# A chunked recurrence with an MLP behind it: the first superstep's triangular inverse in two halves, a second engine that issues DMAs, and a new instruction order

## The chip, the cores and the metric

The kernel runs on one core of one Trainium2 chip. The metric is the device time of one execution in microseconds; the kernel before was run three times (853.11, 855.16 and 856.32 us, median 855.16). A further execution was taken with the hardware profiler. Engines: PE multiplies matrices (into PSUM), DVE, ACT and POOL work element by element, SP issues DMAs. Each engine runs its own instructions strictly in the order in which they were emitted and waits on semaphores for the others.

## The reference

For 4 batches and 8 heads a state of 40x40 goes through 768 time steps; then an MLP with its weights in float64 works on all 3072 tokens:

```python
for t in range(S):
    y[:, :, t] = np.einsum('bhd,bhde->bhe', rt, state)
    Sa = np.einsum('bhde,bhe->bhd', state, at)
    state_decay = state * wt[:, :, None, :] - np.einsum('bhd,bhe->bhde', Sa, bt)
    state = state_decay + np.einsum('bhd,bhe->bhde', vt, kt)
...
x = y.transpose(0, 2, 1, 3).reshape(3072, 320)
h = x @ w_in                                  # 320 x 2048
sp = np.maximum(h, 0.0) + np.log1p(np.exp(-np.abs(h)))
out = (h * erf(sp)) @ w_out                   # 2048 x 320
```

## The kernel before, in words

**Tiling.** The 32 recurrences are worked in two groups of 16, the 768 steps in 6 supersteps of 128 steps, each of 4 chunks of 32 steps. A group's superstep is called q (q0 to q11, the two groups in turn, the second six chunks behind); q0c3 is chunk 3 of the first superstep of the first group. Inside a chunk the recurrence is written as matrix products and one triangular 32x32 solve for each head, so that only the state passes from chunk to chunk.

**Stages of a superstep.**
- `prep` (line 635): a DMA brings the decays w; two scans on DVE (lines 649 and 653) make suffix products (tile Wt) and prefix products (tile Pr).
- `aphase` (662), for each chunk: a DMA (kba) brings k, b and a; `ab` and `bk` (684, 689; DVE or POOL) scale them by the products; `A` (694) makes the chunk's scores on PE in the PSUM tile pA; `Am` (701) masks them into the chunk's Zs tile; two DMAs (AD) write a part of them to DRAM for another layout; `bT` (712) transposes bk through pA, and `bTc` copies that to an sg tile. There are 11 Zs and 11 sg tiles, so scores can be made 11 chunks ahead.
- `tphase` (718), once for all four chunks: DMAs (Ti, Ap) fetch the scores from DRAM, 128 partitions with one 16x16 triangle each; two ACT fills set its border; 14 pairs of a multiply `Tm` (741) and a subtract `Ts` (742) on DVE invert it in place; DMAs write it back (TD) and load it as 32x32 blocks (tb); `R` (750) transposes on DVE; `W` and `DAD` on PE (757) with `Wm` (761) and `Tb` (764) on DVE make the remaining quarter of each block.
- `chain` (767), for each chunk in turn: `Z` (800), the solve `U` (809), copies to SBUF (lines 587 and 589), small DMAs (zu; in q0 copies `zmu`), `PQ` (845) and its mask (848), `MY` (856, 860), and then the new state MT (863) and the outputs Ym (867), which go to DRAM (xw) after chunk 3.
- The MLP for 256 tokens: `load_x` (986) reads the outputs back (xr) and splits them into a high and a low float32r part (xh, xl); `mm1` (1021) makes h out of eight float32r products; `tanh`, `ln`, `exp`, `gelu` on ACT (1029), `nd`, `rho`, `E`, `G` (1053, 1054, 1065, 1066) on DVE or POOL make the activation; `mm2` (1075) multiplies by w_out; `ob` and `out` write the result.
- `weights` (927): 20 DMAs (wd) of float64 weights, each turned into float32 by six instructions (lines 947 to 952: w1 = L947, w3 = L948 and w5 = L952 on DVE, w5 also on POOL; the rest on ACT), those of w_in split into two float32r parts (956, 957, 977, 978).

**The order.** The code only lists operations: `P.add` records name, engine, tiles read and written. The list ORDER (line 17) says in which sequence all 4418 operations are emitted, and the string ENGINES (line 203) gives each its engine: P for PE, A for ACT, V for DVE, G for POOL, S for SP. The lists came out of a planner (`Plan.schedule`, line 303), which is run again only if their lengths don't fit the number of operations. An entry of -1 in ORDER is a filler: a bfloat16 matmul of no use (line 595) that keeps PE at work; there are 288. All 907 DMAs have the letter S:

```python
def dma(self, name, o, i, rd=(), wr=(), pr=0):
    self.P.add(name, "SP", lambda e: self.eng(e).dma_start(o(), i()), rd, wr, pr, ISSUE.get(name, 0.41))
```

For q0, which has no earlier work to hide behind, `aphase` borrows tiles that are not yet in use: chunks 1 to 3 take their kba into Pr[1], Pr[2] and VT[1], and chunks 1 and 3 their scaled a into T. The order within the first microseconds is: a first weight load, the identity, w.q0, kba of chunk 0, and so on; the kba of chunks 2 and 1, and then 3, come later among weight loads.

Of the kernel before, what the change touches and what calls it, by code (L numbers as in the profile page):

```python
# [7 lines left out]
F32 = mybir.dt.float32  # L8
# [7 lines left out]
SCRATCH = 512  # L16
ORDER = (
# [228 lines left out]
LSC = -(0.5 - 2.0 ** -24)  # L246


TICK = 10.24 / 3
FETCH, BLOCK, PHASE = 3.6, 127.3, 94.9  # L250
PAIRS = dict(W=32, DAD=32, mm1=8, mm2=2, A=16, PQ=16, Z=32, U=32, MY=64, pmt=4, UT=2, bT=4, cT=1)
# [9 lines left out]
class Plan:  # L261
# [41 lines left out]
    def schedule(self):  # L303
# [57 lines left out]
        while done < n:  # L361
# [5 lines left out]
            for i in avail:  # L367
                o = ops[i]
                best = None
                for e, d, k in o["alts"]:  # L370
                    if k and lock > now + 1e-9:
                        continue
# [715 lines left out]
def build(tc, I, out, K={}, D=13.5, Dm=27.0, lag=0.0, t0=60.0, amargin=55.0, wpr=40.0, vlag=3.0, tmargin=10.0, verbose=False, emit=True, seq=False, check=True):  # L1088
    with ExitStack() as ctx:
# [17 lines left out]
        def tph(q):  # L1107
            N.tphase(*N.steps[q], pq(q) + 15)
# [117 lines left out]
```

## Time and profile before

| | |
|---|---|
| median of 3 runs (lowest, highest) | 855.16 us (853.11, 856.32) |
| the profiled execution: its time | 849.49 us |
| its span, first to last instruction | 847.7 us |
| mean granted TensorE clock | 0.966 |
| DMA packets; those under 512 bytes | 211459; 165132 |
| DMA bytes, mean rate | 98.96 MB, 117 GB/s |

How to read the views. The page gives for each engine its busy time and its share of the span; a busy PE includes the fillers. The windows give the same for stretches of the span. A row of the timeline is: start, duration, engine, source line, operation, tiles (output<-inputs), shapes, count, and in brackets how long the engine had been idle and who released it. The chain of work that ended last is followed back from the end of the program, at each step to what released it; its rows are start, duration, engine, output tile and line. Rows of DMA issues give count, then shortest, median and longest duration of the issue in ns; that is the time of the issuing engine, not of the transfer. All times below come from the one profiled execution.

### The profile page before, as it was taken

How to read it: one execution, taken by the hardware profiler on the slowest of the kernel's cores; microseconds unless marked ns; L12 is line 12 of the kernel's file. 1: busy time of each engine (PE TensorE's matmuls, PEld its weight loads, DVE VectorE, ACT ScalarE, POOL GpSimd, SP SyncE). 2: the span in 40 equal slices, each digit the busy share in tenths (PEclk: the TensorE clock that was granted, in tenths of full speed). 3: DMA queues.
4: the chain of work that ended last, by engine and by line, in shares of the span. 5: the costliest groups of instructions: out<-in, count | busy, mean ns of one | idle time of the engine just before them, and what ended most of it. 6: DMA issues, size and time to landing. Idle time of an engine off the chain costs nothing.

```text
span 847.7 us, 32375 instructions
## 1 busy us (share of the span) xinstructions
PE 748.0 (88%) x13825; PEld 580.9 (69%) x13825; DVE 628.4 (74%) x1314; ACT 564.3 (67%) x1051; POOL 183.9 (22%) x147
## 2 busy tenths in 40 slices
PE   1798998669888989989999989999899999999986
PEld 1344557656776767777687767888677888787863
DVE  7896664777787779887688786678876778756654
ACT  4552543683658466777488857489775877877992
POOL 2325102144032222110131130211212211023110
PEclk9999999888999999999999979999999999999999
DMA  8857555443564565445536545556446452422000
GB/s 225 248 142 195 123 134 132 99 101 92 133 154 95 126 146 149 105 112 136 123 91 137 120 99 129 136 130 146 100 111 139 111 127 42 107 64 51 22 15 20
DMA packets 211459, 98.96 MB, mean 117 GB/s; under 512 B 165132, under 2 KB 198668, under 8 KB 211308
## 3 DMA queue, kind: packets, MB, share of 16 engines
q1 hardware_dynamic: 211308, 96.81, 48.3%
q8 instruction: 111, 1.82, 0.9%
q14 instruction: 40, 0.33, 0.1%
HBM read 75.07 MB, written 14.16 MB: 105 GB/s over the span
## 4 chain that ended last, share of the span: by engine, by line
PE 46%; DVE 18%; DMA 11%; SPq 9%; ACT 6%; issue 6%; POOL 1%; DVEq 0%; ACTq 0%; POOLq 0%
PE po L1075 13%; PE ph L1021 12%; SPq L592 9%; PE my L856 3%; PE pA L757 3%; DMA Tb<-TD 3%; PE pA L694 3%; PE pQ L845 2%; PE ph L595 2%; ACT r L1029 2%; PE pA L712 2%; DVE Zs L701 2%; DVE h L1066 2%; DVE r L1054 2%; PE my L809 2%
## 5 line engine op out<-in xcount | busy, mean ns | idle before, releaser
L1075 PE MATMUL po<-wo,h 128*128 128x320 f32 x768 | 248.9, 453 | 8.5 <-DVE h L1066 5.3
L1075 PEld LDWEIGHTS po<-wo,h 128*128 128x128 f32 x768 | 135.6, 194 | 50.8 <-DVE h L1066 7.9
L1029 ACT ACTIVATE l<-l 128x512 f32<-128x512 f32 x192 | 112.5, 625 | 22.3 <-DVE nd L1053 20.1
L1021 PE MATMUL ph<-xh,wih 128*128 128x256 f32 x384 | 96.2, 333 | 0.0
L1065 POOL TENSOR_TENSOR l<-l,r 128x512 f32<-128x512 f32 x36 | 50.9, 1418 | 151.0 <-DVE r L1054 61.5
L1021 PE MATMUL ph<-xl,wih 128*128 128x256 f32 x384 | 78.6, 287 | 0.0
L1021 PE MATMUL ph<-xh,wil 128*128 128x256 f32 x384 | 78.4, 286 | 0.0
L1054 DVE SCALAR_TENSOR_TENSOR r<-nd,r 128x512 f32<-128x512 f32 x96 | 69.1, 720 | 10.0 <-POOL nd L1053 8.7
L1066 DVE SCALAR_TENSOR_TENSOR h<-l,h 128x512 f32<-128x512 f32 x96 | 73.1, 770 | 0.6
L1021 PEld LDWEIGHTS ph<-xh,wih 128*128 128x128 f32 x384 | 63.5, 195 | 9.4 <-issue 0.8
L595 PE MATMUL ph<-d 104*128 104x512 bf16 x288 | 69.9, 393 | 0.0
L1029 ACT ACTIVATE l<-h 128x512 f32<-128x512 f32 x96 | 57.3, 626 | 14.4 <-DVE h L589 10.4
L587 ACT COPY h<-ph 128x512 f32<-128x512 f32 x77 | 44.7, 580 | 32.2 <-PE ph L1021 27.3
L856 PE MATMUL my<-Vu,sg 64*40 64x72 f32 x1536 | 51.1, 238 | 14.2 <-ACT Us L587 4.3
L1021 PEld LDWEIGHTS ph<-xh,wil 128*128 128x128 f32 x384 | 61.1, 195 | 0.1
L1021 PEld LDWEIGHTS ph<-xl,wih 128*128 128x128 f32 x384 | 60.9, 195 | 0.1
L684 POOL TENSOR_TENSOR Ab<-bk,Pr 104x512 f32<-104x512 f32 x20 | 25.4, 1269 | 160.8 <-DMA Zs<-Ab 69.2
L1053 DVE TENSOR_TENSOR nd<-l,r 128x512 f32<-128x512 f32 x68 | 49.6, 729 | 14.0 <-ACT r L1029 11.6
L1053 POOL TENSOR_TENSOR nd<-l,r 128x512 f32<-128x512 f32 x28 | 37.7, 1346 | 102.1 <-ACT r L1029 49.4
L856 PEld LDWEIGHTS my<-Vu,sg 64*40 64x40 f32 x1536 | 38.0, 120 | 26.7 <-DVE Vu L848 5.7
L1029 ACT ACTIVATE r<-r 128x512 f32<-128x512 f32 x96 | 55.4, 623 | 0.3
L1029 ACT ACTIVATE r<-l 128x512 f32<-128x512 f32 x96 | 53.6, 618 | 2.4 <-DVE l L1065 2.4
(136 smaller groups left out, 1535.3 us busy)
## 6 DMA issues: line engine op xcount, KB each, us to landing
bk<-in_kba_e SPq DMA_DIRECT2D x45, 416.0 KB
vt<-in_rv_e SPq DMA_DIRECT2D x48, 240.0 KB
wo<-in_moe_w_in SPq DMA_DIRECT2D x10, 512.0 KB
h<-in_moe_w_out SPq DMA_DIRECT2D x10, 512.0 KB
Pr<-in_w_e SPq DMA_DIRECT2D x12, 419.7 KB
Rt<-in_r_e SPq DMA_DIRECT2D x48, 104.0 KB
Zm<-in_v_s SPq DMA_DIRECT2D x48, 80.0 KB
Vu<-in_v_x SPq DMA_DIRECT2D x96, 40.0 KB
```

The costliest lines, as they stand in the source:

```text
L587: self.nc.scalar.copy(o, i)
L592: self.P.add(name, "SP", lambda e: self.eng(e).dma_start(o(), i()), rd, wr, pr, ISSUE.get(name, 0.41))
L595: self.nc.tensor.matmul((self.ph[1], self.pQ)[x], self.d1[:, :128], self.d1[:, :512], start=True, stop=True)
L694: nc.tensor.matmul(pa[i % 2 * 64:i % 2 * 64 + 64, i // 4, i // 2 % 2], bk[:, i].rearrange("p a b -> p (a b)"), ab[:, :, i], start=True, st ...
L856: nc.tensor.matmul(my[h * 64:h * 64 + 40, x, j], sg[xs, j, h], vu[xs, j // 2 * 2 + h, j % 2], start=True, stop=False)
L1021: nc.tensor.matmul(ph[:, j * 256:j * 256 + 256], a[:k, fs], b[:k], start=(m == 0), stop=(m == 7))
L1029: self.P.add(name, "ACT", lambda e: nc.scalar.activation(out=o, in_=i, **kw), rd, wr + ["act"], pr, 0.62)
L1053: P.add("nd", [("DVE", 0.69), ("POOL", 1.28)], lambda e, r=r, l=l, nd=nd: s.eng(e).tensor_tensor(out=nd, in0=l, in1=r, op=ALU.mult), [("l" ...
L1054: P.add("rho", "DVE", lambda e, r=r, nd=nd: nc.vector.scalar_tensor_tensor(out=r, in0=nd, scalar=2 * C4, in1=r, op0=ALU.add, op1=ALU.mult) ...
L1065: P.add("E", [("POOL", 1.28), ("DVE", 0.69)], lambda e: s.eng(e).tensor_tensor(out=l, in0=l, in1=r, op=ALU.mult), [("r", ir)], [("l", il)] ...
L1066: P.add("G", "DVE", lambda e: nc.vector.scalar_tensor_tensor(out=h, in0=l, scalar=-1.0, in1=h, op0=ALU.add, op1=ALU.mult), [("l", il)], [( ...
L1075: nc.tensor.matmul(po, h[:, bs], s.wo[:, f], start=(f == 0), stop=(f == 15))
```

## The change

1. ORDER and ENGINES are new. There are 4458 operations (4418 before) and 155 fillers (288). The letters: S 523 (907), G 548 (143), V 1331 (1274), A 999 (1037), P 1057 (1057). 392 of the 548 with G are DMAs: among them 8 of the 12 w, 34 of the 48 kba, 49 of 96 zs, 33 of 96 AD, 71 of 176 zu, 50 of 96 vx, 27 of 52 TD and tb, 2 of 24 out. The first entries are w.q0 on POOL, then kba.q0c3, rt.q0c0, kba.q0c0, kba.q0c1, tri and kba.q0c2 on POOL with some fills between them; SP's first three are weight loads.
2. SCRATCH, the descriptor memory of DMAs that POOL issues, grows from 512 to 4096 bytes; the rings of Zs and sg tiles shrink from 11 to 10.
3. In q0 only: the scores of the four chunks go to four PSUM banks (pA, ph[0], po[0], po[1]), the transposes to two in turn; chunk 3's scaled a goes to TB[2] instead of T; and `tphase` runs twice, for chunks 0 and 1 and for chunks 2 and 3, on 64 partitions each, with DRAM buffers of their own. The keys by which dependencies are found carry the half. `U` of a chunk waits for its own half alone.
4. The planner gets other costs and rules (AHEAD, ISSUE, HOLD, wop, boost). They act on lists that the planner makes anew; wop and boost are 0.

```diff
-SCRATCH = 512
+SCRATCH = 4096
...
-        self.K = dict(zs=11, ab=1, p=4, sg=11, ...
+        self.K = dict(zs=10, ab=1, p=4, sg=10, ... wop=0.0, boost=0.0)
...
+        s.AD0 = [s.dr.tile([2, 2, NH // 2, 32, 32], F32, name=f"AE{i}") for i in range(2)]
+        s.TD0 = [s.dr.tile([2, 2, NH // 2, 32, 32], F32, name=f"TE{i}") for i in range(2)]
...
-        if q == 0 and c % 2:
+        if q == 0 and c == 1:
             ab, ka = s.T[0][:104].rearrange("p (h a) t -> p h a t", h=2), ("T",)
+        if q == 0 and c == 3:
+            ab, ka = s.TB[2][:104].rearrange("p c q t -> p (c q) t").rearrange("p (h a) t -> p h a t", h=2), ("tb", 2)
...
-        pa = s.pA[:, :256].rearrange("p (y h l t) -> p y l h t", y=2, h=2, t=32)
+        PA, kPA = ((s.pA, "pA"), (s.ph[0], ("ph", 0)), (s.po[0], ("po", 0)), (s.po[1], ("po", 1)))[c if q == 0 else 0]
+        PB, kPB = ((s.pA, "pA"), (s.ph[0], ("ph", 0)))[c % 2 if q == 0 else 0]
+        pa = PA[:, :256].rearrange("p (y h l t) -> p y l h t", y=2, h=2, t=32)
...
-    def tphase(self, g, s_, pr):
+    def tphase(self, g, s_, pr, part=None):
...
+        parts = (0, 1) if part is None else (part,)
+        c0, n = (0, NC) if part is None else (part * 2, 2)
+        nb = NBK * n // NC
+        p0, m0 = part and 64 or 0, n * NQ
+        ps, ms = slice(p0, p0 + 2 * nb), slice(c0 * NQ, c0 * NQ + m0)
+        AD, TD, kAD, kTD = (s.AD[q % 2], s.TD[q % 2], q % 2, (q % 2,)) if part is None else (s.AD0[part], s.TD0[part], 2, (2, part))
+        PW, kPW = (s.ph[0], ("ph", 0)) if part else (s.pA, "pA")
+        tb, W = s.TB[it].rearrange("p c q t -> p (c q) t")[:, ms], s.T[0][:, ms]
...
+        cs = range(c0, c0 + n)
+        key = lambda k, *x: [(k,) + x + (p,) for p in parts]
...
-        P.add("U", "PE", mmu, [("zt", izt)] + [("tb", it, j) for j in range(2)], ["pz"], pr, 0.42)
+        P.add("U", "PE", mmu, [("zt", izt)] + [("tb", it, j, c // 2) for j in range(2)], ["pz"], pr, 0.42)
...
-        todo = [(q, x) for q in range(nst) for x in ("p", 0, 1, 2, 3, "t")]
+        todo = [(q, x) for q in range(nst) for x in (("p", 0, 1, "t0", 2, 3, "t1") if q == 0 else ("p", 0, 1, 2, 3, "t"))]
```

More of the change, by code (lines that the diff above doesn't have):

```diff
@@ L246 @@
 LSC = -(0.5 - 2.0 ** -24)
+AHEAD = 4.0
 TICK = 10.24 / 3
@@ L366, in schedule @@
             rest = []
+            soon = {}
+            for r, j in pend:
+                if r <= now + 0.2 and only[j]:
+                    soon[only[j]] = min(soon.get(only[j], 1e9), ops[j]["pr"])
             for i in avail:
                 o = ops[i]
+                if only[i] in ("DVE", "ACT") and soon.get(only[i], 1e9) < o["pr"] - 3:
+                    rest.append(i)
+                    continue
                 best = None
@@ L371, in schedule @@
                     if k and lock > now + 1e-9:
+                        continue
+                    if e == "SP" and queue > now + AHEAD:
                         continue
@@ L415, in schedule @@
                     start.append(now)
-            nxt = [f for f in list(free.values()) + [lock] + [b[1] for b in bank.values()] if f > now + 1e-9]
+            nxt = [f for f in list(free.values()) + [lock, queue - AHEAD] + [b[1] for b in bank.values()] if f > now + 1e-9]
             if pend:
@@ L732, in tphase @@
-        kt = [("ti", x) for x in range(2)]
-        T = s.TI[:, 16:528].rearrange("p (a b) -> p a b", a=16)
-        for n, o, i in (("T0", s.TI[:, 0:544].rearrange("p (a b) -> p a b", b=32)[:, :, 0:16], s.cst[:, None, :].to_broadcast([128, 17, 16])), ("T1", s.TI[:, 16:528:33], s.cst)):
-            P.add(n, "ACT", lambda e, o=o, i=i, n=n: nc.scalar.activation(out=o, in_=i, func=AF.Copy, scale=0.0 if n == "T0" else 1.0), ["cst"], kt, pr, 0.36 if n == "T0" else 0.22)
-        tm = s.TMP[0]
-        for j in range(1, 15):
-            m, n = j, 15 - j
-            tv_ = tm[:, :m * n].rearrange("p (c i) -> p c i", c=m)
-            d = 0.13 + m * n * 0.00104
-            P.add("Tm", "DVE", lambda e, tv_=tv_, m=m, n=n, j=j: nc.vector.tensor_tensor(out=tv_, in0=T[:, 0:m, j:j + 1].to_broadcast([128, m, n]), in1=T[:, j:j + 1, j + 1:16].to_broadcast([128, m, n]), op=ALU.mult), kt, ["tmp"], pr, d)
-            P.add("Ts", "DVE", lambda e, tv_=tv_, m=m, j=j: nc.vector.tensor_tensor(out=T[:, 0:m, j + 1:16], in0=T[:, 0:m, j + 1:16], in1=tv_, op=ALU.subtract), ["tmp"], kt, pr, d)
+            s.dma("Ap", lambda j=j: AP[j * 64:j * 64 + 64], lambda j=j: avj[j], [("ad", kAD, c, j) for c in cs], key("ap", j), pr)
@@ new lines, in tphase @@
+        kt = key("ti", 0) + key("ti", 1)
+        kap = key("ap", 0) + key("ap", 1)
+        ktm = key("tmp")
+        TI, cst = s.TI[ps], s.cst[ps]
+        T = TI[:, 16:528].rearrange("p (a b) -> p a b", a=16)
+        for nm, o, i in (("T0", TI[:, 0:544].rearrange("p (a b) -> p a b", b=32)[:, :, 0:16], cst[:, None, :].to_broadcast([2 * nb, 17, 16])), ("T1", TI[:, 16:528:33], cst)):
+            P.add(nm, "ACT", lambda e, o=o, i=i, nm=nm: nc.scalar.activation(out=o, in_=i, func=AF.Copy, scale=0.0 if nm == "T0" else 1.0), ["cst"], kt, pr, 0.36 if nm == "T0" else 0.22)
@@ new lines, in tphase @@
+        tm = s.TMP[0][ps]
+        for j in range(1, 15):
+            m, k = j, 15 - j
+            tv_ = tm[:, :m * k].rearrange("p (c i) -> p c i", c=m)
+            d = 0.13 + m * k * 0.00104
+            P.add("Tm", "DVE", lambda e, tv_=tv_, m=m, k=k, j=j: nc.vector.tensor_tensor(out=tv_, in0=T[:, 0:m, j:j + 1].to_broadcast([2 * nb, m, k]), in1=T[:, j:j + 1, j + 1:16].to_broadcast([2 * nb, m, k]), op=ALU.mult), kt, ktm, pr, d)
+            P.add("Ts", "DVE", lambda e, tv_=tv_, m=m, j=j: nc.vector.tensor_tensor(out=T[:, 0:m, j + 1:16], in0=T[:, 0:m, j + 1:16], in1=tv_, op=ALU.subtract), ktm, kt, pr, d)
@@ L751, in tphase @@
-        pw = s.pA.rearrange("p (a b) -> p a b", b=32)
+        P.add("R", "DVE", lambda e: nc.vector.transpose(fl(W), fl(tb)), ktb, s.TK, pr, 0.6 * n / NC)
+        pw = PW.rearrange("p (a b) -> p a b", b=32)[:, :m0]
         def mm(e, l, r, c):
@@ L1172, in ahead @@
                 tag(q)
-                {"p": prep, "t": tph}.get(x, lambda q: aph(q, x))(q)
-        for x in range(6):
+                once(q, x)
+        for _ in range(7):
             q, x = todo.pop(0)
             tag(0)
-            {"p": prep, "t": tph}.get(x, lambda q: aph(q, x))(q)
+            once(q, x)
         N.weights(wpr)
```

127 lines of the change are left out of this document (64 added, 63 removed), and 367 rows, old and new, of the table ORDER.

## The prediction

> **What bounds the kernel now.** I read the page first, for the span and the engines; then the busy time by windows, to cut the span into stages; then, for the one stage where PE does not bound, PE's and DVE's timeline and the chain of work that ended last.
>
> The page, and four windows (columns after the window: length, then PE, PEld, DVE, ACT, POOL busy with instruction counts, the granted clock, the DMA share, GB/s):
>
> ```profile
> span 847.7 us, 32375 instructions
> PE 748.0 (88%) x13825; PEld 580.9 (69%) x13825; DVE 628.4 (74%) x1314; ACT 564.3 (67%) x1051; POOL 183.9 (22%) x147
> ```
>
> ```profile
> 0.00:127.00 127.00, 96.56 (x1336) 52.38 (x1337) 96.55 (x199) 62.07 (x127) 33.98 (x31) 0.97 0.68 178
> 127.00:200.00 73.00, 57.23 (x1355) 48.15 (x1353) 46.96 (x103) 43.18 (x79) 21.15 (x16) 0.86 0.48 109
> 200.00:830.00 630.00, 584.88 (x11106) 474.43 (x11104) 477.65 (x1003) 456.43 (x841) 128.77 (x100) 0.98 0.47 108
> ```
>
> ```profile
> 44.44 29.09 PE L595 MATMUL ph<-d 104*128 104x512 bf16 x134
> 74.18 1.43 PE L757 MATMUL pA<-T,Ap 32*32 32x32 f32 x128 [0.65 <-issue]
> 127.31 0.59 PE L1021 MATMUL ph<-xh,wih 128*128 128x256 f32 x2
> ```
>
> From 200 to 830 us PE is busy 584.88 of 630 (93%): there PE bounds, and only its 45.1 us of idleness, with the 15.8 us between 127 and 200, can be won. The first 127 us are different. PE looks busy, but the 134 matmuls of line 595 are fillers (217 ns apart), which compute nothing. The first MLP matmul (L1021) starts at 127.31; 720.4 us follow. So the place to win is the time of that matmul. DVE is busy 96.55 of the first 127 us (76%) and the DMA engines 68%: neither is full. The chain shows what the head waits for:
>
> ```profile
> 15.89 1.15 PE pA L694 x16
> 42.70 0.43 DVE Zs L701
> 46.80 2.66 DMA Ti<-AD
> 49.48 0.18 DVE tmp L741
> ```
>
> ```profile
> 66.44 2.40 DMA TD<-Ti
> 69.59 3.69 DMA Tb<-TD
> 74.65 1.43 DVE r L947
> 77.75 1.57 DVE wir L978
> 79.36 0.70 DVE T L761
> 83.73 0.46 PE my L809 x32
> ```
>
> The scores of chunk 0 come at 15.89, those of chunk 3 are masked only at 43.13 (the last L701). The inverse of all four starts at 49.48, comes back from DRAM at 73.3, and the first solve U (L809) starts at 83.73; between R and Wm (79.36) DVE does weight conversion (L947, L978) while the path waits.
>
> **The change, the head first.** Where the change puts each instruction I read from its lists ORDER and ENGINES against the sequence of P.add; durations are rows.
>
> *First loads.* Now w.q0 is POOL's first DMA and the four kba loads stand among the next seven.
>
> ```profile
> 0.00:10.00 10.00, 0.00 (x0) 0.00 (x0) 6.07 (x12) 5.49 (x9) 2.50 (x9) 1.00 0.76 206
> 30.00:40.00 10.00, 8.37 (x29) 3.40 (x28) 7.90 (x13) 5.11 (x11) 1.88 (x2) 0.83 0.96 254
> ```
>
> ```profile
> 8.30 2.36 DVE L649 TENSOR_TENSOR_SCAN Wt<-Pr,d 104x516 f32<-104x516 f32 x2 [0.91 <-DMA Pr<-in_w_e]
> ```
>
> ```profile
> 23.05 0.50 SPq L592 DMA_DIRECT2D vt<-in_kba_e  x1
> ```
>
> Before, the scan waited for w.q0 until 8.30, with 0.59 MB (by the tiles' shapes) queued ahead of it; chunk 3's kba was issued only at 23.05. After, SP issues three weight loads (1.57 MB) at once as nothing holds them, beside 2.13 MB on POOL. If the queues share evenly, w.q0 lands with 0.86 MB moved, 4.2 us at 206 GB/s behind some 2 us of start: the scan at about 6 (5 to 8). All 3.7 MB take 14.6 to 18 us at 254 to 206 GB/s. From scan to chunk 0's scores 7.6 us stay (8.30 to 15.89), so 13.6; chunks 0 and 1 are masked by about 18, chunks 2 and 3 by 22 instead of 43. The four PSUM banks alone are small: the wait they take away is this one of the first 127 us.
>
> ```profile
> PE pA L712 <- DVE Zs L701: 3.6, 2, 2.0
> ```
>
> *Inverse in halves.* A half has 64 of 128 partitions but the same row lengths, so each of its 28 multiply and subtract steps costs what a full one costs:
>
> ```profile
> 114.31 0.16 DVE L741 TENSOR_TENSOR tmp<-Ti 128x14 f32<-128x14 f32 x1
> 120.88 0.18 DVE L742 TENSOR_TENSOR Ti<-Ti,tmp 128x14 f32<-128x14 f32 x1
> ```
>
> That is 28 in 6.7 us (0.238 each, one other instruction among them), so the change adds 6.7 us of DVE, eight DMAs, two ACT fills, and 1 us for R, Wm and Tb in two pieces. From the last mask to the first multiply took 6.35 us (43.13 to 49.48); half 0 thus starts at 24.4, and with 46 steps up to its last subtract (the halves alternate) ends at 24.4+10.9=35.3. Then TD and tb: 64.76 to 73.36 before (the rows of TD and Tb above and two below), 8.6; I add 2 because TD is issued by POOL with wlo and w5 in between: R at 46.
>
> ```profile
> 64.58 0.18 DVE L742 TENSOR_TENSOR Ti<-Ti,tmp 128x14 f32<-128x14 f32 x1
> 73.36 0.71 DVE L750 STREAM_TRANSPOSE T<-Tb 128x512 f32<-128x512 f32 x1 [0.45 <-DMA Tb<-TD]
> ```
>
> From R to U took 10.4, of which some 4 were DVE's weight work ahead of Wm; with half-length pieces and less ahead I take 7. **First U at 53 instead of 83.7** (48 to 62).
>
> *From U to the first MLP matmul* the order of work is the old one (four chunks, x to DRAM and back), 43.6 us. But weight conversion that stood ahead of U now stands here: 8 more L948, 5 L947, 2 L952, 2 L978, one more scan, less some copies.
>
> ```profile
> 83.66:127.31 43.65, 40.80 (x781) 23.84 (x780) 29.88 (x80) 22.71 (x56) 5.08 (x4) 1.00 0.53 126
> 40.00:70.00 30.00, 30.00 (x156) 13.99 (x155) 27.77 (x61) 16.59 (x32) 6.86 (x5) 1.00 0.62 161
> ```
>
> ```profile
> L948 DVE SCALAR_TENSOR_TENSOR r<-wo,r 128x512 int32<-128x512 int32 x10 | 10.3, 1030 | 0.2
> L948 DVE SCALAR_TENSOR_TENSOR r<-h,r 128x512 int32<-128x512 int32 x9 | 8.0, 894 | 0.2
> ```
>
> So DVE's 29.88 us grow by about 16 to 46. At the 93% of its fullest stretch (27.77 of 30) that is 50 us; I take 51: **first MLP matmul at 104 instead of 127.3, 23 us saved.** DVE before it sums to 93 us: 96.5 and the halves' 7.7, less some 11 that the order puts behind it (a prefix scan, conversions, copies given to ACT and POOL). That is 90% of 104, so DVE becomes the head's limit. The DMA engines' 0.68 of 127 is 86 us, 83% of 104; a share of 0.96 was seen. PE loses 150 of the 286 fillers ahead of that matmul (133 of 288 in all) and has room.
>
> *POOL as second issuer.* ENGINES gives POOL 392 of 915 DMAs, besides 156 computing instructions (143 before). No row shows a DMA issued by POOL. The nearest are SP's issues, and what POOL takes where DVE does the same:
>
> ```profile
> L592 SPq DMA_DIRECT2D AD<-Zs x96: 303/445/1770, 28.2 to 693.7; - x96
> L592 SPq DMA_DIRECT2D Zs<-Ab x92: 767/835/2317, 16.4 to 749.0; - x92
> L592 SPq DMA_DIRECT2D bk<-in_kba_e x45: 307/390/965, 2.2 to 678.5; - x45
> ```
>
> ```profile
> L1065 POOL TENSOR_TENSOR l<-l,r 128x512 f32<-128x512 f32 x36 | 50.9, 1418 | 151.0 <-DVE r L1054 61.5 <-ACT l L1029 59.8 <-DVE l L1065 15.6
> L1065 DVE TENSOR_TENSOR l<-l,r 128x512 f32<-128x512 f32 x60 | 44.5, 747 | 2.8 <-ACT l L1029 2.4
> ```
>
> Bounds of one issue on POOL: 0.39 us (as SP's cheapest) to 1.77 us (SP's longest AD). At SP's medians POOL's 392 would take 226 us, 0.58 each; POOL is 1.9 times as slow as DVE at equal work, so I take 0.58x1.9=1.1. POOL then works 54x1.1+31=90 us ahead of the first MLP matmul (104 available) and 338x1.1+165=537 in the 690 behind it: it holds, without much room in the head. What is queued behind a POOL DMA that waits is POOL's own nd, E, xl and w5, for which DVE and ACT wait.
>
> *The rest.* One less Zs and sg tile: ten chunks of scores ahead instead of eleven; no wait for either ring is among the longest, so nothing; without that cover, one chunk's pace once. The larger descriptor scratch, the re-keyed dependencies, chunk 3's Ab in Tb's third buffer and the two planner constants of value 0 cost nothing; the planner's new costs don't run, since ENGINES has as many letters as operations. Behind the first MLP matmul the same PE work remains; DVE gets some 20 us more there, ACT about as much less, both with room in the 630 us window. Of PE's waits for landings I count half:
>
> ```profile
> PE my L856 <- DMA Vu<-Us: 3.3, 5, 1.4
> PE my L860 <- DMA Rt<-in_r_e: 2.6, 2, 2.2
> ```
>
> *Sum.* Span 847.7-23-3=821.7; the profiled run took 849.49, 1.8 beyond its span: 823.5. The median shown, 855.16, is 1.0067 times the profiled run, so 829.
>
> **The rivals.** *POOL's issue decides (slower).* At the upper bound, 1.77, POOL needs 31+96=127 us before the first MLP matmul, so nothing is won, and 165+598=763 where 690 are available: span 127+763+30=920, 926 on the median's scale. It decides from about 1.6 us (117+706+30=853). For it: the bounds reach there, and POOL is slow at everything; against it: SP's medians are far below. Own range 862 to 950.
>
> *DVE stays at 76% in the head.* Then 93 us take 122, and with a start at 6 the matmul comes at 126: 853. For it: DVE's in-order queue holds conversions that wait for loads and ACT; against it: the 93% stretch, with the same mix. Range 846 to 857.
>
> *The second queue also frees the steady part.* If small transfers no longer stand behind SP's issues and bulk loads, half of PE's 45 us of idleness goes: 829-22=807. The chain gives SP's issuing 9% and DMA 11%:
>
> ```profile
> PE 46%; DVE 18%; DMA 11%; SPq 9%; ACT 6%; issue 6%; POOL 1%; DVEq 0%; ACTq 0%; POOLq 0%
> ```
>
> The Trainium skill (DMA: Bandwidth & Descriptors, Issuing engines are not separate DMA queues) says that DMAs of all issuers run on the same 16 engines and that issuing from several saves only the sequencer's time, usually small beside the transfer. By that rule this rival is not to be had and 829 stands; the trace shows issues of 0.4 to 0.8 us against 2.4 to 3.7 for TD and Tb, which agrees.
>
> *The change doesn't do what it says* needs ORDER to be discarded; I count 4458 operations and 4458 letters, so no.
>
> **How the numbers follow.** A change of 0.5% (4.3 us) is about what can be told from none. Forecast 0.57 (own range 812 to 846: U from 48 to 62, DVE at 85 to 95%); POOL's issue decides 0.20; DVE at 76% 0.10; steady part freed 0.13. Faster: 0.57+0.13+0.03 of the DVE case; same 0.06 of it; slower 0.20+0.01. The range 806 to 870 leaves out half a tenth below and about 0.15 above.
>
> **What would show it.** L809's first start near 53, L1021's near 104, DVE busy 88 to 93% until then, L649's first scan near 6; 182 instructions each of the multiply and the subtract instead of 168, with a 64-partition form as long as the 128-partition one; POOL's issues near 1.1 us each. Behind it, 200 us after the first MLP matmul, PE at 93%. Wrong if POOL's issues are above 1.6 us, if ACT or DVE wait long for POOL, if DVE's head stays at 76%, or if PE's busy share behind the head moves by more than two points.

## The result and the profile after

The changed kernel takes 891.9 us, the median of 4 runs (887.02 to 895.19), where the kernel before took 854.9 us beside it. The ratio is 1.0429, with a 95% interval of 1.0377 to 1.0482: the change is **slower by 4.3%**. The forecast was 829 us. Sign and size were both wrong, and 891.9 lies above the range (806 to 870). A run more than 1.5% above the fastest of its kernel is left out of every time and ratio below, and the profiled executions of e7 and e13 are such runs.

The page after: the span, the busy times, the queues and the shares of the chain.

```profile
span 889.4 us, 32404 instructions
PE 744.7 (84%) x13692; PEld 583.5 (66%) x13692; DVE 693.7 (78%) x1371; ACT 549.4 (62%) x1013; POOL 437.1 (49%) x552
q1 hardware_dynamic: 119081, 50.91, 24.4%
q0 software_dynamic: 19696, 45.92, 19.1%
PE 38%; DVE 26%; DMA 11%; issue 10%; POOL 7%; ACT 6%; SPq 1%; DVEq 0%; POOLq 0%; ACTq 0%
```

SP's issuing fell from 9% of the chain to 1%. PE's share fell too (46 to 38%); DVE (18 to 26%), issue (6 to 10%) and POOL (1 to 7%) took their place. "Issue" is time in which an engine waited for nothing that the profile shows. DVE's busy time rose by 65 us (628.4 to 693.7); PE does the same 13,537 matmuls of use.

First the head. Two pieces of PE's timeline, then four of DVE's, then two windows of the changed kernel:

```profile
60.69 0.51 PE L835 MATMUL my<-zt,Tb 32*32 32x40 f32 x32
109.92 0.59 PE L1048 MATMUL ph<-xh,wih 128*128 128x256 f32 x2
```

```profile
9.50 2.36 DVE L658 TENSOR_TENSOR_SCAN Wt<-Pr,d 104x516 f32<-104x516 f32 x2 [5.55 <-DMA Pr<-in_w_e]
26.11 0.86 DVE L714 TENSOR_TENSOR Zs<-po,tri 64x256 f32<-64x256 f32 x2 [0.81 <-PE po L707]
30.45 0.16 DVE L767 TENSOR_TENSOR tmp<-Ti 64x14 f32<-64x14 f32 x1
54.54 0.44 DVE L776 STREAM_TRANSPOSE T<-Tb 128x256 f32<-128x256 f32 x1
```

```profile
0.00:110.00 110.00, 67.72 (x1153) 39.12 (x1153) 89.92 (x178) 54.79 (x116) 60.77 (x85) 0.92 0.65 179
200.00:830.00 630.00, 563.54 (x10951) 455.93 (x10941) 494.72 (x1000) 403.53 (x736) 313.52 (x400) 0.94 0.44 108
```

The first solve came 23.0 us earlier than before (60.69 against 83.66), the first MLP matmul 17.4 us earlier (109.92 against 127.31). The second window shows the other side: between 200 and 830 us PE is busy 563.54 us where it was busy 584.88, at a granted clock of 0.94 instead of 0.98.

Where the time went is seen by following the MLP. The table gives the start of the n-th of the 1536 matmuls of its first product (L1021 before, L1048 after), in us, from the two profiled executions:

| n | before | after | difference |
|---|---|---|---|
| 1 | 127.3 | 109.9 | -17.4 |
| 129 | 218.7 | 224.3 | +5.6 |
| 513 | 419.0 | 419.3 | +0.3 |
| 769 | 542.6 | 546.9 | +4.3 |
| 1025 | 649.7 | 686.1 | +36.4 |
| 1281 | 742.0 | 788.9 | +46.9 |
| 1536 | 813.5 | 855.9 | +42.4 |

The head's gain is gone by the 129th matmul; from there to some 520 us the two are level; then the changed kernel falls behind by over 40 us. The windows of that stretch, before and then after:

```profile
500.00:790.00 290.00, 278.35 (x5375) 227.31 (x5375) 211.66 (x463) 217.06 (x401) 55.45 (x44) 0.98 0.46 106
```

```profile
500.00:790.00 290.00, 254.28 (x4782) 202.83 (x4779) 222.53 (x448) 175.19 (x315) 142.98 (x178) 0.92 0.40 98
```

PE was busy 96% of these 290 us and is busy 88%, with 593 of its instructions fewer done. DVE does 15 instructions fewer in 10.9 us more. No engine is full there, ACT and DVE have room, and yet PE waits. The longest of its waits in this stretch (total, times, longest; it does not occur there in the kernel before):

```profile
PE po L1102 <- DVE h L1093: 6.5, 5, 2.1
```

The tile h is the activation that DVE hands to the second product. The groups of the activation's two largest DVE instructions from 500 us on (count, busy, mean ns, idle before), before and then after, and a row of ACT's waits in the same stretch after (total, times, longest), which has no counterpart before:

```profile
L1066 DVE SCALAR_TENSOR_TENSOR h<-l,h 128x512 f32<-128x512 f32 x54 | 38.3, 716 | 0.4
L1054 DVE SCALAR_TENSOR_TENSOR r<-nd,r 128x512 f32<-128x512 f32 x53 | 37.4, 706 | 7.3 <-POOL nd L1053 6.6
```

```profile
L1093 DVE SCALAR_TENSOR_TENSOR h<-l,h 128x512 f32<-128x512 f32 x54 | 46.8, 876 | 3.4 <-POOL l L1092 2.6
L1081 DVE SCALAR_TENSOR_TENSOR r<-nd,r 128x512 f32<-128x512 f32 x52 | 41.0, 789 | 2.2 <-POOL nd L1080 1.3
```

```profile
ACT l L1056 <- POOL nd L1080: 17.6, 5, 6.5
```

The same DVE instruction takes 876 ns where it took 716, and ACT waits 17.6 us for a POOL instruction for which it did not wait in this stretch before. I took each DVE instruction's time above the shortest tenth of its kind, with what POOL did beside it. From 500 us on this lengthening sums to 15.5 us before and 42.1 us after, in the whole run to 54.0 and 101.4 us, nearly all of it beside POOL's arithmetic.

### The profile page after: what moved, and what is told of

The parts are those of the page before. It is cut to its first block, busy times and chain, and to the rows that moved or that the text cites. A ratio compares the mean times of both kernels' runs of the same rounds, so it can differ in the third digit from the quotient of the medians.

```text
span 889.4 us, 32404 instructions
## 1 busy us (share of the span) xinstructions
PE 744.7 (84%) x13692; PEld 583.5 (66%) x13692; DVE 693.7 (78%) x1371; ACT 549.4 (62%) x1013; POOL 437.1 (49%) x552
## 2 busy tenths in 40 slices
DMA packets 138929, 98.98 MB, mean 111 GB/s; under 512 B 98261, under 2 KB 122061, under 8 KB 138777
## 3 DMA queue, kind: packets, MB, share of 16 engines
q1 hardware_dynamic: 119081, 50.91, 24.4%
q0 software_dynamic: 19696, 45.92, 19.1%
## 4 chain that ended last, share of the span: by engine, by line
PE 38%; DVE 26%; DMA 11%; issue 10%; POOL 7%; ACT 6%; SPq 1%; DVEq 0%; POOLq 0%; ACTq 0%
PE po L1102 14%; PE ph L1048 9%; PE my L882 3%; DVE h L1093 3%; DVE r L1081 3%; DVE tmp L767 3%; DVE Ti L768 3%; PE pA L783 2%; DVE nd L1080 2%; DMA xr<-xd 2%; DVE Wt L658 2%; DMA bk<-in_kba_e 2%; PE pQ L871 2%; ACT l L1056 2%; PE pA L707 2%
## 5 line engine op out<-in xcount | busy, mean ns | idle before, releaser
L1102 PE MATMUL po<-wo,h 128*128 128x320 f32 x768 | 257.3, 473 | 19.6 <-DVE h L1093 14.5
L1102 PEld LDWEIGHTS po<-wo,h 128*128 128x128 f32 x768 | 145.0, 204 | 72.4 <-DVE h L1093 19.7
L1048 PE MATMUL ph<-xh,wih 128*128 128x256 f32 x384 | 91.0, 319 | 3.8 <-DVE h L598 2.7
L1093 DVE SCALAR_TENSOR_TENSOR h<-l,h 128x512 f32<-128x512 f32 x96 | 78.2, 823 | 5.2 <-POOL l L1092 4.0
L1048 PE MATMUL ph<-xl,wih 128*128 128x256 f32 x384 | 79.6, 289 | 2.5 <-DVE xl L1032 1.6
L1081 DVE SCALAR_TENSOR_TENSOR r<-nd,r 128x512 f32<-128x512 f32 x96 | 76.6, 798 | 2.9 <-POOL nd L1080 1.3
L1048 PE MATMUL ph<-xh,wil 128*128 128x256 f32 x384 | 78.6, 287 | 0.0
L1048 PEld LDWEIGHTS ph<-xh,wih 128*128 128x128 f32 x384 | 62.4, 197 | 10.5 <-DVE h L598 3.3
L601 POOL DMA_DIRECT2D Vu<-Us x71 | 40.8, 576 | 48.6 <-ACT Us L596 25.7
L707 PE MATMUL pA<-Ab,bk 104*64 104x64 f32 x720 | 33.9, 241 | 36.5 <-DVE bk L700 21.9
L1048 PEld LDWEIGHTS ph<-xl,wih 128*128 128x128 f32 x384 | 61.8, 197 | 2.9 <-DVE xl L1032 1.8
L596 ACT COPY h<-ph 128x512 f32<-128x512 f32 x72 | 41.6, 581 | 33.9 <-PE ph L1048 33.5
L1048 PEld LDWEIGHTS ph<-xh,wil 128*128 128x128 f32 x384 | 61.3, 196 | 0.0
L707 PEld LDWEIGHTS pA<-Ab,bk 104*64 104x64 f32 x720 | 27.8, 149 | 44.5 <-DVE bk L700 20.7
L1048 PE MATMUL ph<-xl,wir 128*128 128x256 f32 x192 | 55.5, 289 | 0.0
L1048 PE MATMUL ph<-xh,wir 128*128 128x256 f32 x192 | 55.4, 289 | 0.0
```

Of the source, the lines that this page charges most:

```text
L596: self.nc.scalar.copy(o, i)
L707: nc.tensor.matmul(pa[i % 2 * 64:i % 2 * 64 + 64, i // 4, i // 2 % 2], bk[:, i].rearrange("p a b -> p (a b)"), ab[:, :, i], start=True, st ...
L1048: nc.tensor.matmul(ph[:, j * 256:j * 256 + 256], a[:k, fs], b[:k], start=(m == 0), stop=(m == 7))
L1081: P.add("rho", "DVE", lambda e, r=r, nd=nd: nc.vector.scalar_tensor_tensor(out=r, in0=nd, scalar=2 * C4, in1=r, op0=ALU.add, op1=ALU.mult) ...
L1093: P.add("G", "DVE", lambda e: nc.vector.scalar_tensor_tensor(out=h, in0=l, scalar=-1.0, in1=h, op0=ALU.add, op1=ALU.mult), [("l", il)], [( ...
L1102: nc.tensor.matmul(po, h[:, bs], s.wo[:, f], start=(f == 0), stop=(f == 15))
```

## The experiments

Each ran beside the kernel before; the ratio is to that. The edits are shown in short, against the kernel that each starts from; lists of entries are written as what was done to them. The four kernels with the old order and transfers on POOL (e4, e7, e8, e10) and the two with the new head (e5, e6) have 768 bytes of descriptor memory; e18 has the rings and the 4096 bytes that are shown for e15.

**e1, e2: the new order with one issuer.** The transfers of POOL go back to SP, all of them (e1) or those behind the first MLP matmul (e2):

```diff
-ENGINES: 392 DMAs "G", 523 "S"
+ENGINES: 915 DMAs "S"                      (e1)
+ENGINES: 54 DMAs "G" up to the first mm1, 861 "S"   (e2)
```

> The changed kernel with its own order, halves, banks and rings, but with all 915 transfers issued by SyncE again. Theory Q (queue): the loss of about 60 us behind the first MLP matmul (109.9 us against 127.3 us there, 42.9 us late at the end) comes from transfers that stand in GpSimd's queue and hold GpSimd's element-wise work and each other. Then most of it goes: 830 to 855 us. Theory P (port): VectorE loses 101 us beside GpSimd's element-wise work where it lost 54 us, because the new order places that work beside VectorE's; that work stays, so 880 to 895 us. Theory O (order): the new order was laid out for two issuing engines; one engine then issues 915 transfers of about 0.6 us, 549 us in all, in an order that doesn't suit it: 890 us or more.

> The changed kernel with its order; the 54 transfers that GpSimd issues ahead of the first MLP matmul stay on GpSimd, the 338 behind it go to SyncE. Theory Q: the 17 us won ahead of the first MLP matmul stay and most of the loss behind it goes: 830 to 850 us, the fastest of the four. Theory P: 880 to 895 us. Theory O: 885 us or more, as with all on SyncE, with the first MLP matmul still near 110 us.

Measured: 950.2 us (1.116, 1.1045 to 1.1276) and 954.4 us (1.1219, 1.1097 to 1.1341). Theories Q and P fell, theory O holds: with all transfers on SP the new order is 58 us slower still. It is not the amount of issuing: SP's 915 issues took 563.0 us in e1, its 907 in the kernel before 568.7. Whether POOL's queue costs something of its own in the new order is not shown, since e1 and e2 move its transfers onto SP's. e1 also shows that the second issuer was not needed for the head: in e1 the first solve came at 61.7 and the first MLP matmul at 111.4 us. The Trainium skill (DMA: Bandwidth & Descriptors, Issuing engines are not separate DMA queues) says that a second issuer saves only the sequencer's issue time, usually small beside the transfer. For each transfer the traces agree (0.63 us an issue on POOL against 4.4 us to landing for its kba loads), but in this order the second issuer is worth 58 us in all.

**e3: no arithmetic on POOL behind the first MLP matmul.**

```diff
-ENGINES: ab, bk, MTs, nd, E, xl, w5, wr1 behind the first mm1: 127 "G"
+ENGINES: the same 127 "V"
```

> The changed kernel with its order and its transfers; the 127 element-wise instructions that GpSimd has behind the first MLP matmul are done by VectorE, at the same places of the order. Theory P: VectorE's 128 us beside GpSimd's work shrink; it takes on 127 instructions of about 0.7 us (89 us) and is freed of some 80 us of lengthening, so it stays near 700 us busy, and the span falls to 860 to 880 us. Theory Q: a transfer that waits in GpSimd's queue now holds only other transfers; 860 to 890 us, so this run alone does not tell Q from P. Theory O: VectorE is the busier engine and the order is not made for it: 890 to 910 us.

Measured: 912.2 us (1.0682, 1.0547 to 1.0818), 2 us above theory O's range; theory P fell. DVE's lengthening fell from 101.4 to 24.5 us and DVE's busy time from 693.7 to 688.3, and yet it is 20 us slower. So the lengthening can't simply be taken off the time: in this order POOL's help is worth more than the lengthening that comes with it.

**e4, e7, e8: the old order with two issuers.** The kernel before, with those transfers on POOL that the change puts there (e4), only the loads among them (e7), only the results (e8):

```diff
-SCRATCH = 512
+SCRATCH = 768
-ENGINES: 907 DMAs "S"
+ENGINES: 359 DMAs "G"                      (e4)
+ENGINES: 158 DMAs "G": kba w rv rt vx zv wd tri msk      (e7)
+ENGINES: 201 DMAs "G": zs AD Ti TD zu xw xr out          (e8)
```

> The kernel before with its own order and 11 score tiles; 359 of the transfers that the change gives to GpSimd are issued by GpSimd here too (all of that list but Ap and tb, for which the descriptor memory of 768 bytes that fits here is too small). Theory Q: the transfers wait in GpSimd's queue among its element-wise work as in the changed kernel: 875 to 900 us. Theory P: the order of the element-wise work is that of before, 850 to 865 us. Theory O: the order of before is not at fault, 845 to 865 us. If the small descriptor memory binds, the transfers on GpSimd take over 1 us each instead of 0.5 to 0.75 us.

> The kernel before in its own order; of the 359 transfers that GpSimd issued in the earlier run only the 158 loads from the inputs (kba, w, rv, rt, vx, zv, wd, constants) stay on GpSimd. They wait for buffers that come free, not for results. Theory Q (transfers that wait for results hold what stands behind them in GpSimd's queue): a small part of the 92 us, 855 to 880 us. Theory M (any transfer moved off its place in the matched order costs about the same, 0.26 us each): 41 us, 890 to 900 us.

> The kernel before in its own order; only the 201 transfers of results (zs, AD, Ti, TD, zu, xw, xr, out) on GpSimd. Theory Q: most of the 92 us, 910 to 940 us. Theory M: 0.26 us each, 51 us, 900 to 912 us.

Measured: 946.1 us (1.1114, 1.0977 to 1.1251), 919.7 us (1.0736, 1.0652 to 1.082), 883.6 us (1.0347, 1.0284 to 1.0411). e4 lies above the ranges of all three theories, and both theories of e7 and e8 missed the split: the loads, which wait for no result, cost 67 us for 158 transfers, the results 31 us for 201. In e4 an issue on POOL took 0.61 us (219.6 us for 359), as in the changed kernel, and not the 1 us that was to show that the smaller descriptor memory binds.

**e9, e10: why the loads cost so much.** The old order without POOL's arithmetic (e9), and the same with the loads on POOL (e10):

```diff
-ENGINES: 115 element-wise "G" behind the first mm1
+ENGINES: the same 115 "V"                  (e9, e10)
+ENGINES: 158 DMAs "G" as in e7             (e10)
```

> The kernel before in its own order with all transfers on SyncE; its 115 element-wise instructions of GpSimd behind the first MLP matmul are done by VectorE, at the same places of the order. It is the base for the next run. VectorE takes on 115 instructions of about 0.7 us (80 us) and loses some 45 us of its 54 us of lengthening: 35 us more work on an engine that is busy 76% there. By all theories 865 to 895 us.

> The run before this one with the 158 loads on GpSimd, which there has no element-wise work behind the first MLP matmul. Theory Q (in GpSimd's one queue a load that waits for its buffer holds the element-wise work behind it, and that work holds the loads): with that work gone the loads cost little, within 15 us of the run before this one, where they cost 68 us in the kernel before. Theory T (transfers of GpSimd's queue are themselves the worse ones, or disturb those of SyncE): they cost 50 to 70 us here too.

| old order | all transfers on SP | 158 loads on POOL | the loads cost |
|---|---|---|---|
| POOL's arithmetic as before | 853.0 | 919.7 (1.0736) | 67 us |
| 115 instructions given to DVE | 872.1 (1.0178, 1.0099 to 1.0256) | 878.3 (1.0264, 1.0194 to 1.0334) | 6 us |

This is the clearest result, as theory Q has it: in the old order the loads on POOL cost 6 us, which is not clear of the noise, where POOL does not compute behind the first MLP matmul, and 0.4 us each on average where it does. The rows suggest how. POOL's waits in e7, then in e10, then DVE's waits for POOL in e7 (in the kernel before the first of these was 8.7 us, and the second was not among the longest):

```profile
POOL Zm L592 <- PE my L800: 25.3, 7, 8.1
POOL Vu L592 <- PE my L860: 25.5, 6, 7.2
```

```profile
POOL Zm L592 <- PE my L800: 137.0, 14, 30.4
POOL Vu L592 <- PE my L860: 101.7, 12, 35.4
```

```profile
DVE r L1054 <- POOL nd L1053: 19.3, 8, 8.0
DVE h L1066 <- POOL l L1065: 16.5, 5, 5.4
```

A load waits until PE has read the old contents of its buffer. In e10 POOL stands 137.0 us for Zm's buffers and nobody minds, since only further loads stand behind. In e7 the arithmetic (nd, E) stands behind such a load, DVE waits for it, and with DVE the matmul that frees the buffer. This chain is read from the waits and argued: DVE's waits for these two grew by some 27 us, and the loads cost 67.

**e5, e6: the new head, the old rest.** Against the changed kernel: the first 648 entries of the new ORDER, and behind them whatever is left in the old sequence, on the old engines and all on SP; in e6 the head's transfers are on SP too:

```diff
+ORDER = new[:648] + [x for x in old if x not in new[:648]]
-self.K = dict(zs=10, ab=1, p=4, sg=10, ...
+self.K = dict(zs=11, ab=1, p=4, sg=11, ...
```

> The changed kernel's first 648 entries, up to its first MLP matmul, with its halves, its four PSUM banks and GpSimd's 54 transfers there; behind them whatever is left, in the sequence and on the engines of the kernel before, all transfers on SyncE; 11 score tiles. Theory O (the new order behind the head is the worse one): the head's gain of 17 us stays but for some 10 us of work on VectorE and ScalarE that the new head leaves undone at its first MLP matmul (weight conversions, the third superstep's scan): 838 to 850 us. Theory M (an order and its queues are matched to each other to within a microsecond, and a splice breaks that, as moving the transfers did): 870 to 950 us. First MLP matmul near 110 us by both.

> As the run before, but all transfers of the head on SyncE too, so that GpSimd issues none. Theory O and theory M both expect the same time as that run within 5 us, since with all on SyncE the changed kernel's first MLP matmul came at 111.4 us against 109.9 us. If GpSimd's issuing is what made the head faster, the first MLP matmul comes near 127 us and the time is 10 to 17 us above that run.

Measured: e5 867.1 us (1.0159, 1.0091 to 1.0228), e6 859.3 us (1.0046, 0.9999 to 1.0093). With the halves, the four banks and the new sequence of the head, e6 is no faster than the kernel before. Its timeline and its first window:

```profile
60.89 0.49 PE L835 MATMUL my<-zt,Tb 32*32 32x40 f32 x32
128.85 0.80 PE L1048 MATMUL ph<-xh,wih 128*128 128x256 f32 x2
```

```profile
0.00:128.00 128.00, 65.60 (x1156) 38.31 (x1156) 100.01 (x220) 62.08 (x131) 35.87 (x38) 0.90 0.68 179
```

The first solve is as early as in the changed kernel, and the first MLP matmul comes at 128.85, no earlier than before. Where the rest follows the old sequence, all that stood ahead of that matmul is done ahead of it, DVE does 100.01 us of work in 128 (78%), and the early solve buys nothing. Both expectations had the first MLP matmul near 110 us, and both missed; the times lie between the two theories. POOL's issuing is not what was lacking in e6: in e5, which has it in the head, that matmul came at 133.63.

**e15: the old head, the new rest.** Against the kernel before:

```diff
+ORDER = old[:first mm1] + [x for x in new if x not in old[:first mm1]]
-self.K = dict(zs=11, ab=1, p=4, sg=11, ...
+self.K = dict(zs=10, ab=1, p=4, sg=10, ...
-SCRATCH = 512
+SCRATCH = 4096
```

> The complement of the run with the new head and the old rest: the kernel before up to its first MLP matmul (one inverse for the first superstep, all transfers on SyncE), and behind it what is left in the sequence, on the engines and with the two queues of the changed kernel; 10 score tiles. Theory R (the new rest loses the time, whatever stands ahead of it): it loses against the kernel before what the changed kernel loses behind its head, 35 to 60 us: 888 to 915 us. Theory M (only a splice is at fault): the new head and old rest lost 8 to 14 us by their splice; here as much, 862 to 870 us.

Measured: 899.3 us (1.054, 1.0487 to 1.0593), 45 us above the kernel before. The new rest, with its two issuers, loses the time whatever stands ahead of it.

**e16, e17, e18: where in the rest.** New up to 500 us and old behind (e16), the same at 640 us (e17), old up to 500 us and new behind (e18); the old part has all its transfers on SP, the new part its two issuers:

```diff
+ORDER = new[:at 500 us] + [x for x in old if x not in new[:at 500 us]]      (e16; e17 at 640 us)
+ORDER = old[:at 500 us] + [x for x in new if x not in old[:at 500 us]]      (e18)
```

> The changed kernel up to the entry that TensorE reaches at 500 us in its profile, and behind it what is left in the old sequence, on the old engines, all transfers on SyncE. In the profiles the changed kernel stands level with the kernel before until about 520 us and falls 42.9 us behind in the 370 us after that. Theory S (the loss is made in the new sequence behind 500 us): 855 to 870 us, no more than a splice's 8 to 14 us above the kernel before. Theory D (the new sequence has put off work by 500 us, which then has to be done): 880 to 900 us although the rest is the old one.

> As the run before, spliced at 640 us. At 640 us the changed kernel's profile is 9 to 25 us behind. Theory S: 870 to 885 us. Theory D: 885 to 900 us, as with the splice at 500 us.

> The complement: the kernel before up to the entry that TensorE reaches at 500 us in its profile, with all transfers on SyncE, and behind it what is left in the new sequence with its two issuing engines; 10 score tiles. Theory S: the last 350 us alone lose it: 890 to 910 us. Theory D: nothing was put off by 500 us, so the new sequence loses little from there: 860 to 875 us.

Measured: e16 867.7 us (1.0112, 1.0044 to 1.018), e17 886.8 us (1.0322, 1.0241 to 1.0403), e18 895.0 us (1.0448, 1.0385 to 1.0511). e16 and e18 are as theory S has it and outside theory D's ranges: most of the loss is made behind 500 us, by the new rest, and little of it was put off to be paid later. e17 lies 2 us above S's range and inside D's, and does not tell the two apart. The window of e16 that answers to those above, and the groups of e16 and of e18:

```profile
500.00:790.00 290.00, 268.74 (x5287) 220.62 (x5288) 212.28 (x462) 206.17 (x384) 54.26 (x48) 0.95 0.47 108
L1093 DVE SCALAR_TENSOR_TENSOR h<-l,h 128x512 f32<-128x512 f32 x56 | 41.0, 740 | 0.5
L1081 DVE SCALAR_TENSOR_TENSOR r<-nd,r 128x512 f32<-128x512 f32 x53 | 38.1, 719 | 7.5 <-POOL nd L1080 6.8
```

```profile
L1066 DVE SCALAR_TENSOR_TENSOR h<-l,h 128x512 f32<-128x512 f32 x56 | 49.8, 900 | 3.4 <-POOL l L1065 2.6
ACT l L1029 <- POOL nd L1053: 17.5, 5, 6.3
```

From 500 us on DVE's lengthening is 16.1 us in e16 and 38.5 in e18: it goes and comes with the new sequence, and so do ACT's wait for POOL's nd and PE's wait for h (none in e16 from 500 to 790 us, 6.6 us in e18). So does a wait that is not for POOL, ACT's for the recurrence's pQ: from 500 us on 2.9 us before, 33.5 in the changed kernel, 6.6 in e16 and 27.9 in e18.

**e11, e12: parts of the new order's transfers back to SP**, the 158 loads (e11) or the 234 results (e12):

```diff
-ENGINES: 392 DMAs "G"
+ENGINES: 234 DMAs "G", the results         (e11)
+ENGINES: 158 DMAs "G", the loads           (e12)
```

> The changed kernel in its own order; its 158 loads on GpSimd go back to SyncE, the 234 transfers of results stay on GpSimd. Theory L (loads on GpSimd are the dear ones in any order): faster than the changed kernel, 860 to 885 us. Theory M (the order is matched to where each transfer is issued; 392 moved ones cost 58 us): 158 moved ones cost about 23 us, 910 to 920 us.

> The changed kernel in its own order; the 234 transfers of results that GpSimd issues go to SyncE, its 158 loads stay. Theory L: slower than the changed kernel by what the results on SyncE's crowded queue cost, 920 to 950 us, well above the run with the loads on SyncE. Theory M: 234 moved ones cost about 35 us, 920 to 930 us.

Measured: 919.0 us (1.0809, 1.0738 to 1.088) and 938.7 us (1.0986, 1.0917 to 1.1056). e11 refutes theory L: in the new order the loads are not the dear ones on POOL (e12 lies in L's range and 9 us above M's). Both groups cost time where they leave the queue for which the order was laid out, 27 us for 158 and 47 us for 234.

**e13, e14: is it the clock?** Short fillers into PE's idle places, in the changed kernel (e13, 473 in 64 places) and in the kernel before (e14, 240 in 49); they write columns of the PSUM tile my that nothing reads:

```diff
+(self.my[:, 1, 288:512], self.d1[:, :128], self.d1[:, :224])
+ORDER: -3 (one such filler), int((idle - 0.1) / 0.13) times ahead of each
+       PE operation that idled 0.4 us or longer
```

> The changed kernel with 473 short fillers more, in 64 places between 110 and 840 us where TensorE stood idle 0.4 us or longer in its profile, so many in each as fill the idle time; nothing else waits for them. Without them 36 stretches of 3.4 us ran at half the TensorE clock (18 before), nearly all behind a stretch in which TensorE was busy under half of the time, and the same 13,537 matmuls of use took 700.3 us where they took 678.1 us before. Theory C (the lost clock is a cause of its own: 22 us of the 42 us): half the half-clock stretches go, the matmuls of use come down by 10 us or more, and the time falls by 8 to 20 us, to 872 to 884 us. Theory W (the waits come first and TensorE is not what the chain waits for there; the clock is only their sign): the granted clock rises, the time stays within 5 us of 891.9 us.

> The kernel before with 240 short fillers more, in 49 places between 127 and 800 us where TensorE stood idle 0.4 us or longer in its profile. Theory C: it has 14 half-clock stretches there, of 1.7 us lost each; if half of them go, 843 to 849 us, a version faster than both. Theory W: 850 to 858 us.

Measured: e13 886.2 us (1.036, 1.0295 to 1.0426), 5.7 us below the changed kernel, with intervals that overlap; e14 868.5 us (1.0167, 1.0119 to 1.0215), above the ranges of both theories. The clock of the changed kernel, then of e13:

```profile
core 0: 889.4 us, clock 0.931
```

```profile
core 0: 890.4 us, clock 0.960
```

The clock rose nearly to that of the kernel before (0.966), PE's matmuls of use came down by 20 us in sum, and the time came down by 5.7 us, which the intervals do not tell from none and which lies between the two theories (W: within 5 us; C: 8 to 20 less). So raising the clock this way does not win back the 37 us. That the clock costs nothing is not shown: e14's fillers cost 14 us in the kernel before, so in e13 a gain may be hidden behind what the fillers cost. No version run here is faster than the kernel before.

## Why the prediction was wrong, point by point

- **First loads: wrong.** The first scan began at 9.50, not near 6 and later than before (8.30), though w.q0 is POOL's first DMA. By then some 2.3 MB had moved (the rates of the first 10 us), where I had it land with 0.86 MB moved: the loads issued beside it got more of the rate than an even share. With all transfers on SP (e1 and e6) the first scan began at 5.16 and 4.94.
- **Scores and inverse: mechanism right, late.** The last mask of the four chunks ended at 26.97 (forecast 22, before 43.13), half 0 began at 30.45 (24.4), its R at 54.54 (46), the first U at 60.69 (53; my bounds 48 to 62 hold it).
- **Halves: right.** There are 182 multiplies and 182 subtracts, and the 64-partition form took 0.16 to 0.21 us, as the full one.
- **First MLP matmul at 104: it came at 109.92.** DVE was busy 89.92 of 110 (82%; forecast 90%).
- **"23 us saved" carried to the end: this is the step that failed first.** I took the first MLP matmul as the end of the head, and its shift as a shift of the whole. It is only a place in the sequence. The new order gets there sooner partly by putting work behind it (I counted some 11 us on DVE and still subtracted the full 23), and by the 129th matmul the 17.4 us are gone. e6, which does that work at its old place, has the first solve at 60.89 and gains nothing. The rival "DVE stays at 76% in the head" described e6 well (78%; it priced 853 us, e6 took 859.3); I gave it 0.10.
- **"The same PE work remains" behind it: this step cost the sign.** I held the work unchanged and so the time. The work did stay, but its sequence was new, and I priced that at -3 us. e15 and e18 put the loss there: 45 us for the new rest, 37 us for its part behind 500 us. A new sequence of 4458 operations was the largest part of the change, and I had no term for it.
- **POOL's price: too high.** I took 1.1 us an issue, by POOL's slowness in arithmetic; it took 0.63 (247.5 us for 392), near SP's own medians. Two rows of issues:

```profile
L601 POOL DMA_DIRECT2D Vu<-Us x71 | 40.8, 576 | 48.6 <-ACT Us L596 25.7 <-DVE Us L598 22.6 <-issue 0.2
L601 POOL DMA_DIRECT2D Zs<-Ab x45 | 31.0, 690 | 10.7 <-POOL Ab L695 4.7 <-DVE Ab L695 4.2 <-issue 0.8
```

- **The slower rival: its side right, its mechanism wrong.** 891.9 lies in its own range (862 to 950), but it was to decide from 1.6 us an issue, and 0.63 is far below. POOL's time is not short (437.1 of 889.4 us busy). In the old order a POOL queue which both waits for buffers and computes is dear; how much of the changed kernel's loss comes from that is open. I had named what is queued behind a waiting POOL DMA (nd, E, xl, w5) and then priced only the issue, not the wait. e7, e9 and e10 show the price in the old order: 67 us with the arithmetic, 6 without.
- **The second issuer frees the steady part: no.** SPq fell from 9% to 1% of the chain and PE's busy share from 93% to 89% between 200 and 830 us.
- **A sign that was ill chosen.** "93% in the 200 us behind the first MLP matmul" was read from 200 to 830 us. In the 200 us behind its first MLP matmul the kernel before has 168.45 us of PE (84%), the changed one 165.42 (83%).

**What stays open.** Shown is that most of the loss lies in the new rest behind 500 us (e15, e16, e18), that a higher clock by fillers does not win it back (e13), and that the new order needs its two issuers (e1, e2, e11, e12). "The new rest" is its sequence together with its engines and its two issuers; no run has the new sequence on the old engines. With it go 26.6 us more of DVE's lengthening, 17.6 us of ACT's wait for POOL's nd and 30.6 us more of ACT's waits for pQ. Whether any of these is the cause is not shown: e3 took POOL's arithmetic behind the first MLP matmul away and lost 20 us more, and no run kept it on POOL without the collisions. That would need another order.

## What to carry to other kernels

In a kernel with a hand-laid order, moving an instruction to another queue is a change of order for everything behind it there: price what stands behind each wait, not the instruction. In the old order, transfers that wait for buffers did little harm on an engine that had nothing else to do (6 us) and much on one that computed (67 us); in the new one, laid out for two issuers, the same loads were better left on the computing engine (e11). A milestone's shift counts only if the same work has been done by then: compare the remaining work at both milestones before carrying the difference to the end.

## What the runs showed of the hardware

**DVE beside POOL.** In the changed kernel 460 DVE instructions ran beside POOL's issuing of DMAs alone: 225.8 us, lengthened by 2.9. Beside POOL's arithmetic it depends on the operands: 93 that read PSUM took 42.4 us, lengthened by 0.6; 137 with two SBUF inputs took 171.3 us, lengthened by 80.8 (before: 90 of them, 102.7 us, lengthened by 41.0). The extreme case, DVE's and then POOL's timeline:

```profile
65.73 7.60 DVE L658 TENSOR_TENSOR_SCAN Wt<-Pr,d 104x516 f32<-104x516 f32 x2
```

```profile
67.29 1.28 POOL L983 TENSOR_TENSOR wil<-l,wih 128x512 fp32r<-128x512 f32 x1
68.52 2.50 POOL L978 TENSOR_TENSOR l<-l,r 128x512 f32<-128x512 f32 x2
70.97 1.27 POOL L983 TENSOR_TENSOR wil<-l,wih 128x512 fp32r<-128x512 f32 x1
```

Two scans that take 2.36 us at 9.50 took 7.60: four POOL instructions back to back, 67.29 to 72.24, kept the second out until they were done. The Trainium skill (SBUF — State Buffer, Who interferes with whom) says that a DVE instruction with two SBUF inputs and a GpSimd instruction that reads SBUF exclude each other for a whole instruction, and that one with at most one SBUF input contends only in the two-port modes, which copies, casts and `tensor_scalar` can enter. The traces agree as far as they go: the scans above have two SBUF inputs, and copies from SBUF to SBUF, with one, are held up too; in which mode these ran no trace shows. Seven copies of MT beside POOL's arithmetic took 5.89 us in the changed kernel, where one by itself takes 0.31 to 0.32; an example, DVE's and then POOL's timeline:

```profile
631.59 1.35 DVE L598 COPY Zm<-MT 40x320 f32<-40x320 f32 x1
```

```profile
631.47 1.29 POOL L1092 TENSOR_TENSOR l<-l,r 128x512 f32<-128x512 f32 x1 [2.88 <-ACT l L1056]
```

So which DVE instruction an order puts beside POOL's arithmetic matters: the new order put 137 of those with two SBUF inputs there, the old one 90.

**The clock.** The trace's clock records show 3.4 us stretches at half speed, 36 in the changed kernel after the first 20 us and 18 before. In these two traces every stretch at full speed followed one in which PE was busy at least 50%; two thirds of those at half speed (35 of 54) followed one below 55%, the others one above it.

**Packets.** POOL's 45.92 MB went in 19,696 packets (2.3 KB each), SP's 50.91 MB in 119,081 (0.43 KB); all packets fell from 211,459 to 138,929, and the time did not follow.
